# Decoding the weights of an attention kernel with feed-forward to 24 bits: three bitwise steps on VectorE, and the low part by a subtraction on GpSimd

## The chip, the core and the metric

The kernel runs on one core of a Trainium2 chip. The metric is the device time of one launch in microseconds (us), as the median of several runs. A profile of one execution goes with it. TensorE multiplies matrices, VectorE (DVE in the profile), ScalarE (ACT) and GpSimd (POOL) work on vectors, and SyncE (SP) issues the loads and stores. Each engine executes its own instructions in the order in which they stand in its queue, and waits on semaphores for the others.

## What is computed

Linear attention with positive random features for 8 batches, 8 heads, 576 positions and a head dimension of 64, followed by a feed-forward layer on all 4608 tokens of width 512 and inner width 2048. Cut to what matters:

```python
def phi(x):
    proj = np.einsum('bhsd,md->bhsm', x, omega)
    h = proj - np.sum(x * x, axis=-1, keepdims=True) / 2.0
    return np.exp(h - np.max(h, axis=-1, keepdims=True)) / np.sqrt(m)
q_p, k_p = phi(q * scale), phi(k * scale)
kv = np.einsum('bhsm,bhsd->bhmd', k_p, v)
num = np.einsum('bhsm,bhmd->bhsd', q_p, kv)
den = np.einsum('bhsm,bhm->bhs', q_p, k_p.sum(axis=2))[..., None] + 1e-06
x = (num / den).transpose(0, 2, 1, 3).reshape(B * S, H * D)
h = x @ w_in
out = (h - np.tanh(h)) @ w_out
```

The inputs q, k, v and omega are 32-bit floats. The weights `w_in` and `w_out` are 64-bit floats.

## The kernel before

**Tiles.** The inner width of 2048 is cut into 16 chunks of 128 columns, numbered f = 0 to 15. A chunk's weights are 128 partitions by 1024 words of 64 bits: 512 columns of `w_in` and 512 of `w_out`. They come as raw 64-bit words (`raw`, one load of 1 MB each, `fetch`, line 422) and are decoded on the chip, in place, to two 32-bit tiles: a high part `wt[f][:, 0]` and a low part `wt[f][:, 1]`, both in the type fp32r that TensorE multiplies. The products of x and w are made in three passes: xh·wh, xl·wh and xh·wl, where x is split into `xh` and `xl` likewise.

**Order of the work.** 4608 tokens are 18 chunks of 256. At the start the attention of batches 0 and 1 runs: k units (`k_unit`, line 170) make the features of the keys and their sums, q units (`q_unit`, line 319) the features of the queries and a quarter of x each, ending in `x_split` (line 408), which writes a piece of `xh` on ScalarE and of `xl` on VectorE. Eight such pieces (four for each of token chunks 0 and 1) make the x of the first feed-forward pass, which works on both token chunks at once, 512 columns wide. Its step s (`step`, line 545) takes weight chunk s: 12 products into a PSUM tile `h` (line 471), then `g = h - tanh(h)` split into `gh` and `gl` by ScalarE and VectorE (lines 475 to 478), then 12 products into four PSUM tiles (lines 489 to 491). After the 16 steps the remaining token chunks follow, 256 columns wide, with the attention of the later batches in between.

**Decoding.** `decode(f)` (line 427) takes the upper 32 bits of each word (`top`) and 16 middle bits (`mid`). ScalarE writes the absolute value of `top`, seen as a 32-bit float, to a tile `a` (line 438), and 128 times `mid` to a tile `m` (line 440). A clamp (line 442) runs on VectorE for the chunks 0 and 1, on GpSimd for the others. VectorE shifts and masks `a` (line 444), puts in sign and exponent (445), builds the low bits in `m` (448), keeps of `a` the exponent alone (453), and multiplies the two to the low part (454). ScalarE copies `a` to the high part (452). `a` has two buffers, `m` one. The tiles are 128 x 1024.

**What sets the order.** The program is written as one sequence with a count of beats (`t`): a chunk's decode is placed when t reaches 4 + 2.5 f (line 563), and the units by a table. A scheduler of the programming layer (it is on, line 664) then moves instructions of each engine, by its own estimate of when their operands are ready. The loads keep their written order while the first stage runs. The chunks 10 to 15 have their place in memory where the tiles of the first attention stage were, so that their loads follow its end (line 558).

Of the kernel before, what the change touches and what calls it, by code (L numbers as in the profile page):

```python
# [8 lines left out]
F32 = mybir.dt.float32  # L9
F32R = mybir.dt.float32r  # L10
U64 = mybir.dt.uint64
U32 = mybir.dt.uint32
U16 = mybir.dt.uint16
AF = mybir.ActivationFunctionType
ALU = mybir.AluOpType
AX = mybir.AxisListType
# [2 lines left out]
NT, DM, DFF = B * S, H * D, 2048  # L19
P = 128  # L20
# [11 lines left out]
def favor_attention_ffn(ctx: ExitStack, tc: tile.TileContext, qT, kT, va, vt, omT, w, out):  # L32
# [12 lines left out]
    nc = tc.nc  # L45
# [8 lines left out]
    def open_pool(name, side="right"):  # L54
        pools[name] = tc.tile_pool(name=name, bufs=1, side=side, reuse_waits="tile")
        return pools[name].__enter__()
# [37 lines left out]
    dec = open_pool("dec")  # L94
# [318 lines left out]
    wt = {}  # L413

    raws = {}
# [11 lines left out]
    def decode(f):  # L427


        top = raws[f].bitcast(U32)[:, 1::2]  # L430
        topf = raws[f].bitcast(F32)[:, 1::2]
        mid = raws[f].bitcast(U16)[:, 1::4]
        a = dec.tile([P, 2 * DM], U32, tag="a", name=f"a{f}", bufs=2)
        m = dec.tile([P, 2 * DM], U32, tag="m", name=f"m{f}", bufs=1)

        nc.scalar.activation(a.bitcast(F32), topf, AF.Abs)  # L438

        nc.scalar.activation(m, mid, AF.Copy, scale=128.0)  # L440
        engine = nc.vector if f < 2 else nc.gpsimd
        engine.tensor_scalar(a.bitcast(F32), a.bitcast(F32), 2.0**-15, 122879.9921875,  # L442
                             op0=ALU.max, op1=ALU.min)
        nc.vector.tensor_scalar(a, a, 3, 0x3FFFF000, op0=ALU.logical_shift_left, op1=ALU.bitwise_and)
        nc.vector.scalar_tensor_tensor(out=a, in0=top, scalar=0xC0000000, in1=a,
                                       op0=ALU.bitwise_and, op1=ALU.bitwise_or)

        nc.vector.scalar_tensor_tensor(out=m, in0=top, scalar=23, in1=m,
                                       op0=ALU.logical_shift_left, op1=ALU.bitwise_or)

        wt[f] = places[f].tile([P, 2, 2 * DM], F32R, tag=f"w{f}", name=f"w{f}")
        nc.scalar.copy(wt[f][:, 0], a.bitcast(F32))
        nc.vector.tensor_scalar(a, a, 0xFF800000, None, op0=ALU.bitwise_and)
        nc.vector.scalar_tensor_tensor(out=wt[f][:, 1], in0=m, scalar=2.0**-43, in1=a.bitcast(F32),
                                       op0=ALU.mult, op1=ALU.mult)

    xh, xl = [sb.tile([P, 2, NC, TC], F32R, name=f"x{k}") for k in "hl"]
# [95 lines left out]
    while decoded < NF:  # L555
        if t in (2, 4):
            fetch(int(t == 4))
        if not gens and not start and len(places) < NF:
            close_pool("a0")
            weight_places(open_pool("w1", "left"), range(10, NF))  # L560
            for f in range(decoded, decoded + 2):
                fetch(f)
        if decoded in raws and t >= 4 + 2.5 * min(decoded, 16) + 2 * max(0, decoded - 16):
            decode(decoded)
            decoded += 1
            fetch(decoded + 2 - 1)
        if t == 15:
            mode.update(pj=["pj0", "pj1", "po1"], pk=["pk"], pt=["pt", "po0"])
        if done + 2 < decoded and t >= 23 + 1 * done:
            if done == 0:  # L570
                assert xdone[0] == xdone[1] == NC
                out_tiles(0, ("po0", "po1", "pj1", "pt"))
                mode.update(pj=["pj0"], pk=["pk"], pt=["pk"])
            step(done)
            done += 1
        tick(start.pop(t, ()))
        t += 1
# [89 lines left out]
```

## Time and profile before

| | us |
|---|---|
| median of 3 runs | 1066.88 (1065.81 to 1067.43) |
| span of the profiled execution | 1065.4 |
| TensorE products busy in it | 1041.8 (98%) |
| VectorE | 855.5 (80%) |
| ScalarE | 696.4 (65%) |
| GpSimd | 325.9 (31%) |
| weights decoded (first line 438 to last line 454) | 13.0 to 157.7 |

The profiled execution has no other time of its own than its span, from its first instruction to its last; the median of the runs is 1.5 us above it. A row of the profile gives the source line, the engine, the operation, the tile it writes and those it reads, and the shape. In rows with a time in front the first number is the start in us from the start of the span, the second the duration; `[1.06 <-DVE g L476]` says that the engine sat idle for 1.06 us before, until VectorE's `g` of line 476 was done. `min/median/max` are durations in ns. The duration of a VectorE row overlaps the next by about 0.08 us.

### The profile page before, as it was taken

To read this page: it belongs to the slowest core of one execution; us is meant where nothing else is said; L and a number is where in the kernel's file an instruction comes from. 1 tells how busy PE (TensorE), PEld (TensorE's weight loads), DVE (VectorE), ACT (ScalarE), POOL (GpSimd) and SP (SyncE) were. 2 spreads that over 40 slices of the span, in tenths; PEclk is the share of its full clock that TensorE was granted. 3 is DMA by queue.
4 is the path that set the end of the run, shared out by engine and by line. 5 is a ranking of instruction groups with operands and counts; after the bars stand their busy time and mean duration, and the time that the engine had idled before them with its cause. 6 is when DMAs were issued, how large, how long until landed. Compare 5 with 4: busy or idle time off the path is not lost.

```text
span 1065.4 us, 20130 instructions
## 1 busy us (share of the span) xinstructions
PE 1041.8 (98%) x6760; PEld 945.6 (89%) x6760; DVE 855.5 (80%) x2910; ACT 696.4 (65%) x1773; POOL 325.9 (31%) x553
## 2 busy tenths in 40 slices
PE   7988999999999999999999999999999999999998
PEld 7766888999889999999999998999999999999997
DVE  5999995889998886789889878998888887666522
ACT  6997655777677665577777766677767675555422
POOL 4634541344333420133333344333333331000000
PEclk9999999999999999999999999999999999999999
DMA  8750401111111110011111111111101110000000
GB/s 265 237 213 3 187 1 42 53 39 46 31 53 33 54 33 31 11 53 33 53 34 53 34 37 44 33 53 29 47 25 49 33 37 11 30 16 21 1 21 21
DMA packets 35528, 55.90 MB, mean 52 GB/s; under 512 B 12256, under 2 KB 21600, under 8 KB 33376
## 3 DMA queue, kind: packets, MB, share of 16 engines
q1 hardware_dynamic: 35344, 54.57, 16.3%
q8 instruction: 54, 0.88, 0.3%
q14 instruction: 50, 0.41, 0.1%
q10 hardware_dynamic: 80, 0.03, 0.0%
HBM read 45.15 MB, written 9.44 MB: 51 GB/s over the span
## 4 chain that ended last, share of the span: by engine, by line
PE 61%; DVE 2%; ACT 1%; POOL 1%; issue 0%; DVEq 0%; POOLq 0%
PE h L471 26%; PE po L489 8%; PE po L490 8%; PE po L491 8%; PE pj_q L142 2%; PE pk L266 2%; PE pt L366 2%; PE pn L397 1%; PE pn L396 1%; PE pj_kb L142 1%; PE pj_ka L142 1%; PE pk L304 0%; PE pk L302 0%; DVE junk L347 0%; POOL khl L250 0%
## 5 line engine op out<-in xcount | busy, mean ns | idle before, releaser
L471 PE MATMUL h<-xh,w 128*128 128x256 f32 (+1 forms) x2176 | 450.1, 290 | 3.9 <-DVE g L476 2.1
L471 PEld LDWEIGHTS h<-xh,w 128*128 128x128 f32 x2176 | 354.8, 190 | 14.7 <-DVE g L476 3.2
L471 PE MATMUL h<-xl,w 128*128 128x256 f32 (+1 forms) x1088 | 315.8, 290 | 0.0
L489 PE MATMUL po<-w,gh 128*128 128x512 f32 x544 | 213.7, 393 | 0.0
L490 PE MATMUL po<-w,gh 128*128 128x512 f32 x544 | 213.3, 392 | 0.0
L471 PEld LDWEIGHTS h<-xl,w 128*128 128x128 f32 x1088 | 206.9, 190 | 6.0
L491 PE MATMUL po<-w,gl 128*128 128x512 f32 x544 | 209.2, 391 | 0.0
L477 ACT CAST gh<-g 128x512 fp32r<-128x512 f32 x144 | 89.4, 621 | 92.8 <-DVE g L476 91.3
L475 ACT ACTIVATE g<-h 128x512 f32<-128x512 f32 x144 | 85.4, 593 | 95.0 <-PE h L471 82.7
L476 DVE TENSOR_TENSOR g<-h,g 128x512 f32<-128x512 f32 x144 | 98.7, 686 | 57.8 <-ACT g L475 56.6
L478 DVE TENSOR_TENSOR gl<-g,gh 128x512 fp32r<-128x512 f32 x144 | 108.2, 751 | 34.9 <-ACT gh L477 33.1
L491 PEld LDWEIGHTS po<-w,gl 128*128 128x128 f32 x544 | 102.1, 188 | 20.5
L489 PEld LDWEIGHTS po<-w,gh 128*128 128x128 f32 x544 | 102.5, 188 | 16.2
L490 PEld LDWEIGHTS po<-w,gh 128*128 128x128 f32 x544 | 102.5, 188 | 15.3
L347 DVE CUSTOM_DVE_ANT_0 junk<-phi_q,zb 128x128 f32<-128x128 f32 (+1 forms) x320 | 98.5, 309 | 14.4 <-ACT phi_q L150 0.5
L150 ACT ACTIVATE phi_q<-phi_q,nb_q 128x128 f32<-128x128 f32 x240 | 79.6, 392 | 6.8 <-DVE nb_q L146 6.7
L442 POOL TENSOR_SCALAR a<-a 128x1024 f32<-128x1024 f32 x14 | 58.7, 4194 | 54.6 <-ACT a L438 37.2
L250 POOL TENSOR_TENSOR khl<-phi_ka,khl 128x256 fp32r<-128x256 f32 x48 | 37.9, 796 | 121.6 <-DVE khl L249 92.5
L258 POOL CAST vhl<-v 128x128 fp32r<-128x128 f32 (+1 forms) x144 | 45.8, 319 | 91.9 <-PE pk L266 71.5
L390 DVE TENSOR_TENSOR ql<-pt,qh 128x512 fp32r<-128x512 f32 x60 | 41.1, 685 | 32.3 <-ACT qh L389 31.8
L146 DVE CUSTOM_DVE_ANT_0 phi_q<-pj_q,phi_q 128x128 f32<-128x128 f32 x240 | 56.0, 283 | 2.3 <-ACT phi_q L143 2.2
L389 ACT CAST qh<-pt 128x512 fp32r<-128x512 f32 x60 | 34.9, 581 | 32.9 <-PE pt L366 32.6
(152 smaller groups left out, 1938.2 us busy)
## 6 DMA issues: line engine op xcount, KB each, us to landing
raw<-w SPq DMA_DIRECT2D x16, 1024.0 KB, 7.3
kf<-kT SPq DMA_DIRECT2D x32, 288.0 KB, 2.9
qf<-qT SPq DMA_DIRECT2D x72, 128.0 KB, 2.1
out<-o SPq DMA_DIRECT2D x36, 256.0 KB, 2.0
v<-vt SPq DMA_DIRECT2D x24, 288.0 KB, 2.8
v<-va SPq DMA_DIRECT2D x8, 288.0 KB, 5.9
omf<-omT ACTq DMA_DIRECT2D x1, 32.0 KB, 2.2
omf<-omT SPq DMA_DIRECT2D x1, 32.0 KB, 2.4
```

Source lines behind the costliest of these rows:

```text
L146: nc.vector.tensor_tensor_reduce(ph[:, j], pj[:, i, :M], ph[:, j], scale=-SCALE, scalar=3.0e38, op0=ALU.add, op1=ALU.min, accum_out=nb[:, ...
L150: nc.scalar.activation(ph[:, j], ph[:, j], AF.Exp, bias=nb[:, j : j + 1], scale=-1.0)
L347: nc.vector.tensor_tensor_reduce(bank("junk")[r], ph[r, i], kvs[b, c][1][r, h], scale=1.0, scalar=EPS, op0=ALU.mult, op1=ALU.add, accum_ou ...
L442: engine.tensor_scalar(a.bitcast(F32), a.bitcast(F32), 2.0**-15, 122879.9921875, op0=ALU.max, op1=ALU.min)
L471: nc.tensor.matmul(o, w_, x, start=i == 0, stop=i == len(prods) - 1)
L475: nc.scalar.activation(g, p, AF.Tanh)
L476: nc.vector.tensor_sub(g, p, g)
L477: nc.scalar.copy(gh, g)
L478: nc.vector.tensor_sub(gl, g, gh.bitcast(F32))
L489: nc.tensor.matmul(po[t], h, wt[f][:, 0, DM:], start=first, stop=False)
L490: nc.tensor.matmul(po[t], h, wt[f][:, 1, DM:], start=False, stop=False)
L491: nc.tensor.matmul(po[t], l, wt[f][:, 0, DM:], start=False, stop=last)
```

## The change

Only `decode` is changed. The tile `m` and the middle bits go away, and with them ScalarE's second pass (line 440) and VectorE's instructions of the lines 448, 453 and 454. The mask of the shift keeps all bits that the shift leaves. A third bitwise VectorE instruction puts in the three uppermost bits of the lower word (`low`), so that `a` is the weight cut to 24 significant bits. ScalarE's copy rounds it to fp32r as the high part, and the low part is `a` minus that high part: a subtraction on VectorE for the chunks 0 and 1, on GpSimd for the others, 128 x 1024 each. `a` has three buffers instead of two. In the clamp minimum and maximum change places.

```diff
-        mid = raws[f].bitcast(U16)[:, 1::4]
-        a = dec.tile([P, 2 * DM], U32, tag="a", name=f"a{f}", bufs=2)
-        m = dec.tile([P, 2 * DM], U32, tag="m", name=f"m{f}", bufs=1)
-        nc.scalar.activation(a.bitcast(F32), topf, AF.Abs)
-        nc.scalar.activation(m, mid, AF.Copy, scale=128.0)
+        low = raws[f].bitcast(U32)[:, 0::2]
+        a = dec.tile([P, 2 * DM], U32, tag="a", name=f"a{f}", bufs=3)
+        af = a.bitcast(F32)
+        nc.scalar.activation(af, topf, AF.Abs)
         engine = nc.vector if f < 2 else nc.gpsimd
-        engine.tensor_scalar(a.bitcast(F32), a.bitcast(F32), 2.0**-15, 122879.9921875,
-                             op0=ALU.max, op1=ALU.min)
-        nc.vector.tensor_scalar(a, a, 3, 0x3FFFF000, op0=ALU.logical_shift_left, op1=ALU.bitwise_and)
+        engine.tensor_scalar(af, af, 122879.9921875, 2.0**-15, op0=ALU.min, op1=ALU.max)
+        nc.vector.tensor_scalar(a, a, 3, 0x3FFFFFF8, op0=ALU.logical_shift_left, op1=ALU.bitwise_and)
         nc.vector.scalar_tensor_tensor(out=a, in0=top, scalar=0xC0000000, in1=a,
                                        op0=ALU.bitwise_and, op1=ALU.bitwise_or)
-        nc.vector.scalar_tensor_tensor(out=m, in0=top, scalar=23, in1=m,
-                                       op0=ALU.logical_shift_left, op1=ALU.bitwise_or)
+        nc.vector.scalar_tensor_tensor(out=a, in0=low, scalar=29, in1=a,
+                                       op0=ALU.logical_shift_right, op1=ALU.bitwise_or)
         wt[f] = places[f].tile([P, 2, 2 * DM], F32R, tag=f"w{f}", name=f"w{f}")
-        nc.scalar.copy(wt[f][:, 0], a.bitcast(F32))
-        nc.vector.tensor_scalar(a, a, 0xFF800000, None, op0=ALU.bitwise_and)
-        nc.vector.scalar_tensor_tensor(out=wt[f][:, 1], in0=m, scalar=2.0**-43, in1=a.bitcast(F32),
-                                       op0=ALU.mult, op1=ALU.mult)
+        nc.scalar.copy(wt[f][:, 0], af)
+        engine.tensor_sub(wt[f][:, 1], af, wt[f][:, 0].bitcast(F32))
```

The changed kernel's lines up to `decode` have numbers one lower (xl is line 409 instead of 410), those behind it twelve lower. In its `decode` the absolute value is line 434, the clamp 436, the shift 437, the other two bitwise steps 438 and 440, the copy 443 and the subtraction 444.

The scheduler moves the rest. On GpSimd, in the middle of the first attention stage, this stood in a row before (a4 is the `a` tile of chunk 4, and so on; the L442 rows are clamps, `kd` and `vd` small copies of the k units):

```order
L442 TENSOR_SCALAR a4_734<-a4_734 128x1024
L184 COPY kd1_126<-kf_1_3_799 64x64 x2
L185 COPY vd1_127<-v1_125 64x66 x2
L442 TENSOR_SCALAR a5_896<-a5_896 128x1024
L442 TENSOR_SCALAR a6_975<-a6_975 128x1024
L442 TENSOR_SCALAR a7_1072<-a7_1072 128x1024
```

In the changed kernel, from the clamp of chunk 5 to that of chunk 9 (L436 are clamps, L444 subtractions, w3 the weights of chunk 3):

```order
L436 TENSOR_SCALAR a5_881<-a5_881 128x1024
L184 COPY vd0_124<-v0_122 64x66 x2
L444 TENSOR_TENSOR w3_601<-a3_595,w3_601 128x1024
L183 COPY kd1_126<-kf_1_3_784 64x64 x2
L184 COPY vd1_127<-v1_125 64x66 x2
L444 TENSOR_TENSOR w4_728<-a4_722,w4_728 128x1024
L436 TENSOR_SCALAR a6_957<-a6_957 128x1024
L444 TENSOR_TENSOR w5_887<-a5_881,w5_887 128x1024
L436 TENSOR_SCALAR a7_1051<-a7_1051 128x1024
L436 TENSOR_SCALAR a8_1103<-a8_1103 128x1024
L444 TENSOR_TENSOR w6_963<-a6_957,w6_963 128x1024
L436 TENSOR_SCALAR a9_1210<-a9_1210 128x1024
```

The subtractions stand between the clamps, two or three chunks behind them, and the clamp of chunk 5 has come ahead of the copies of the last k unit.

On VectorE, these are the rows from the seventh to the eighth and last `xl` piece of the first two token chunks, before (L454 is the last step of a chunk's decode, here chunk 5; the rest belongs to the attention):

```order
L410 TENSOR_TENSOR xl_101<-pn_0_3_762,xh_100 128x256
L454 SCALAR_TENSOR_TENSOR w5_904<-m5_897,a5_896 128x1024
L350 RECIPROCAL dn_2_1_945<-dn_2_1_945 128x4
L347 ISA junk_65,dn_2_2_1018<-phi_q2_2_1008,zb_1_2_959 128x128
L347 ISA dn_2_2_1018 128x1
L215 TENSOR_TENSOR kvw_1_3_996<-pk_1_3_961,kvw_1_3_996 128x128
L410 TENSOR_TENSOR xl_101<-pn_1_3_872,xh_100 128x256
```

and in the changed kernel (L440 is VectorE's last step of a chunk, here chunk 9):

```order
L409 TENSOR_TENSOR xl_101<-pn_0_3_747,xh_100 128x256
L346 ISA junk1_105,dn_2_2_997<-phi_q2_2_987,zb_0_2_446 64x128
L346 ISA dn_2_2_997 64x1
L214 TENSOR_TENSOR kvw_1_3_975<-pk_1_3_943,kvw_1_3_975 128x128
L349 RECIPROCAL dn_2_1_927<-dn_2_1_927 128x4
L346 ISA junk_65,dn_2_2_997<-phi_q2_2_987,zb_1_2_941 128x128
L346 ISA dn_2_2_997 128x1
L440 SCALAR_TENSOR_TENSOR a9_1210<-raw9_1060,a9_1210 128x1024
L409 TENSOR_TENSOR xl_101<-pn_1_3_857,xh_100 128x256
```

At the same piece of x, VectorE's order had chunk 5 finished and two steps of chunk 6 done before; now it has chunk 9 finished. SyncE's order is unchanged up to the loads of chunk 15.

1 line of the change is left out of this document (removed).

## The prediction

> **What bounds the kernel now.** I read the page's busy times first.
>
> ```profile
> span 1065.4 us, 20130 instructions
> PE 1041.8 (98%) x6760; PEld 945.6 (89%) x6760; DVE 855.5 (80%) x2910; ACT 696.4 (65%) x1773; POOL 325.9 (31%) x553
> ```
>
> TensorE is busy 98% of the span. The work the change takes from VectorE and ScalarE can therefore pay only where TensorE is idle, 1065.4 − 1041.8 = 23.6 us in all. The windows view says where that idle time lies; its columns are the window, its length, and then the busy time and the count of each engine.
>
> ```profile
> 0.00:84.00 84.00, 70.17 (x382) 58.17 (x383) 72.53 (x212) 69.14 (x201) 37.02 (x64) 0.98 0.71 227
> 84.00:100.00 16.00, 13.87 (x75) 11.60 (x74) 15.71 (x42) 12.39 (x24) 8.78 (x2) 1.00 0.01 1
> 100.00:165.00 65.00, 65.00 (x292) 53.61 (x291) 57.66 (x71) 40.88 (x53) 31.23 (x9) 1.00 0.20 80
> 165.00:1066.00 901.00, 892.73 (x6016) 822.23 (x6015) 709.66 (x2588) 573.97 (x1495) 248.83 (x478) 1.00 0.12 35
> ```
>
> TensorE idles 13.8 us before 84 us and 2.1 us up to 100 us; from 100 to 165 us, while the rest of the weights are decoded, it never idles. So a decode that finishes earlier after 100 us is worth nothing, and only the start, where the attention of the first chunks of tokens runs beside the first decodes, is open. Which engine sets the pace there is in the same view of finer windows:
>
> ```profile
> 25.00:50.00 25.00, 23.21 (x132) 19.34 (x132) 25.00 (x68) 24.52 (x74) 16.20 (x15) 1.00 0.82 241
> 50.00:75.00 25.00, 21.07 (x111) 16.59 (x110) 24.95 (x87) 24.58 (x76) 8.20 (x6) 1.00 0.57 195
> 75.00:84.00 9.00, 6.60 (x39) 5.03 (x39) 8.75 (x38) 5.48 (x16) 0.86 (x1) 1.00 0.33 135
> ```
>
> VectorE (third of the busy times) works 58.7 of these 59 us, ScalarE (fourth) nearly as much, GpSimd (fifth) half or less. The feed-forward can start once x is whole, which the `xl` rows of the timeline mark:
>
> ```profile
> 83.04 0.41 DVE L410 TENSOR_TENSOR xl<-pn,xh 128x256 fp32r<-128x256 f32 x1
> ...
> 83.51 0.50 PE L471 MATMUL h<-xh,w 128*128 128x512 f32 x1 [0.23 <-DVE xl L410]
> ...
> 84.98 0.41 DVE L410 TENSOR_TENSOR xl<-pn,xh 128x256 fp32r<-128x256 f32 x1
> ...
> 89.82 0.50 PE L471 MATMUL h<-xh,w 128*128 128x512 f32 x1 [1.06 <-DVE g L476]
> ...
> 97.93 0.50 PE L471 MATMUL h<-xh,w 128*128 128x512 f32 x1 [1.07 <-DVE g L476]
> ```
>
> At 83 to 85 us VectorE writes the last two of the eight `xl` pieces, TensorE takes them up at once, and then waits only twice more, both times for VectorE. VectorE is an in-order engine that is full, so the sum of what stands ahead of the eighth `xl` in its order sets when TensorE becomes full. That is the number I forecast.
>
> **VectorE's own decode work ahead of that point.** The decode rows of VectorE up to 84 us, grouped (count, busy us, mean ns):
>
> ```profile
> L445 DVE SCALAR_TENSOR_TENSOR a<-raw,a 128x1024 uint32<-128x1024 uint32 x7 | 8.5, 1215 | 0.0
> L448 DVE SCALAR_TENSOR_TENSOR m<-raw,m 128x1024 uint32<-128x1024 uint32 x6 | 8.2, 1360 | 0.0
> L454 DVE SCALAR_TENSOR_TENSOR w<-m,a 128x1024 fp32r<-128x1024 uint32 x6 | 7.3, 1215 | 0.0
> L444 DVE TENSOR_SCALAR a<-a 128x1024 uint32<-128x1024 uint32 x7 | 4.8, 686 | 0.1
> L453 DVE TENSOR_SCALAR a<-a 128x1024 uint32<-128x1024 uint32 x6 | 4.2, 692 | 0.0
> L442 DVE TENSOR_SCALAR a<-a 128x1024 f32<-128x1024 f32 x2 | 1.4, 694 | 0.8 <-ACT a L438 0.8
> ```
>
> These are 34.4 us for six whole chunks and the start of a seventh, the same 34 instructions that the order has ahead of the eighth `xl`. The removed instructions (L453, L454) and the new third one (a SCALAR_TENSOR_TENSOR like L445) make a chunk 2 × 1.215 + 0.686 = 3.1 us where it was 3 × 1.215 + 0.686 + 0.692 = 5.0. But the order of the changed kernel has ten whole chunks ahead of the same `xl`. That is 10 × 3.1 = 31.2, plus the two clamps, 1.4, plus the two subtractions of chunks 0 and 1, which stay on VectorE. The nearest row for one of them is L454, also 1024 elements to fp32r: 2 × 1.215 = 2.4. Sum 35.0 us, and from the 34.4 I take 0.9 first, by which the six L448 exceed 1215 ns (that is waiting, treated below): **+1.5 us**. So the saving on VectorE is spent on decoding four chunks earlier than TensorE needs them. ScalarE, by the same count, has 10 absolute values and 9 copies there, where it had 7 absolute values, 6 middle words and 6 copies: 19 and 19, no gain.
>
> **What GpSimd's subtractions cost VectorE.** No row of before has GpSimd subtract 1024 columns. The nearest rows, durations as min/median/max in ns:
>
> ```profile
> L250 POOL TENSOR_TENSOR khl<-phi_ka,khl x48: 727/742/1311, 179.7 to 872.3; 128x256 fp32r<-128x256 f32 x48
> L272 POOL TENSOR_TENSOR zs<-zt x48: 452/508/950, 186.9 to 886.6; 128x128 f32<-128x128 f32 x48
> L249 DVE CAST khl<-phi_ka x48: 263/287/844, 179.2 to 871.4; 128x256 fp32r<-128x256 f32 x48
> L442 POOL TENSOR_SCALAR a<-a x14: 3622/4180/4645, 26.4 to 146.4; 128x1024 f32<-128x1024 f32 x14
> L448 DVE SCALAR_TENSOR_TENSOR m<-raw,m x16: 1204/1217/2057, 15.5 to 153.0; 128x1024 uint32<-128x1024 uint32 x16
> L162 DVE TENSOR_REDUCE nb_k<-pj_k x16: 673/679/692, 6.7 to 64.8; 128x4 f32<-128x512 f32 x16
> ```
>
> By the minima, 128 more columns of a GpSimd tensor-tensor take 727 − 452 = 275 ns, so 1024 columns take 0.73 + 6 × 0.275 = 2.38 us (estimate from L250 and L272; between 2.4 and the 4.2 of the clamp). VectorE is held meanwhile. The timeline has one L448 that starts 0.41 us after a clamp does:
>
> ```profile
> 34.53 3.98 POOL L442 TENSOR_SCALAR a<-a 128x1024 f32<-128x1024 f32 x1 [1.53 <-issue]
> ...
> 34.94 2.06 DVE L448 SCALAR_TENSOR_TENSOR m<-raw,m 128x1024 uint32<-128x1024 uint32 x1
> ```
>
> The L448 takes 2.06 us instead of 1.22: 0.84 us held by a GpSimd read of 1 × 1024 columns. The cast L249 that runs beside the subtraction L250 reaches 0.84 instead of 0.29: 0.56 us held by a read of 2 × 256. L162, which reads PSUM, never varies, so an instruction between may hide part. Scaled by columns like its length, the hold of a subtraction of 2 × 1024 is up to 0.56 + 6 × 0.275 = 2.2 us; twice the clamp's would be 1.7; with PSUM readers in front it can be 0. I take 1.3, three quarters of the 1.7. GpSimd's order has the subtractions of chunks 2 to 8 ahead of the point, seven: **+9.1 us** (0 to 15.4). The order also has the clamps of chunks 2 to 9 there, eight, where before has five:
>
> ```profile
> 0.00:85.00 85.00, 1.39 (x2) 19.85 (x5) 0.98 0.70 224
> ```
>
> (the window of L442 alone; POOL is the last pair.) Three more at up to 0.84: **+1.5** (0 to 2.5).
>
> The Trainium skill, page "SBUF — State Buffer", section "Who interferes with whom", says more: GpSimd shares a port pair with VectorE, and a VectorE instruction with two SBUF inputs, or in a two-port mode, is fully blocked until a GpSimd instruction that reads SBUF and started first is finished. The clamp rows disagree as to the whole length (4.18 us long, 0.84 held); the L250 rows come closer (0.56 of 0.74). By that rule each subtraction would hold VectorE 2.38 us, seven 16.7 us, and the sum below would be 17.6 instead of 10.0.
>
> **What is won.** After the point, before still decodes on VectorE between the `g` rows, and TensorE loses the 2.1 us of the 84:100 window. In the changed order no decode stands there until chunk 10, whose words cannot be loaded before the attention's tiles are free: **−1.5** (0 to −2.1). In the first 25 us VectorE has gaps that an earlier chunk can fill: **−0.6** (0 to −1).
>
> **Edits that I cost at nothing.** All that leaves ScalarE and VectorE after 100 us: TensorE is full there. The third `a` buffer lifts the wait of ScalarE's absolute value, which nothing waits for there either. The six subtractions of chunks 10 to 15 hold VectorE too, but TensorE then has a product of another step to do, and if that cover is gone each costs at most 2.2 us. GpSimd's small copies `kd` and `vd` queue behind more, at the worst a clamp and a subtraction, 6.6 us; what waits for them is a projection whose result VectorE, full as it is, takes up late anyway. Without that cover this goes to the high end. SP issues the same loads in the same order up to chunk 15. Swapping min and max in the clamp: the same row. TensorE's order differs in places up to the 2,059th of its 6,760 products and is then the same; up to there I take ±1 us.
>
> **Sum:** 1.5 + 9.1 + 1.5 − 1.5 − 0.6 = +10.0 us on the profiled execution, 1065.4 to 1075.4 us. The runs' median, 1066.88, lies 1.5 us above that span, so I forecast 1066.9 + 10 = **1076.9 us**. A measurement of this kernel tells about 0.2%, 2.1 us, from no change.
>
> **Rivals.**
> - *A, the forecast:* the subtractions hold VectorE in its full stage. Between 1071 and 1085 us. Chance 0.64.
> - *B, the holds fall on instructions that wait anyway or read PSUM:* then 1.5 − 2.1 − 1 = −1.6 to about +2, 1065 to 1069 us. For it: L162 is untouched by GpSimd and makes up 19 of the 84 us. Against: the L448 and L249 maxima. Chance 0.15: 0.06 faster, 0.06 the same, 0.03 slower.
> - *C, faster:* the attention stage is set by VectorE's work per chunk and not by where the scheduler put the chunks: six chunks × 1.9 us saved, less 2.4 for two subtractions, is 9.1 us of the 13.8 that TensorE idles, 1058 us. It decides if VectorE's decode instructions let attention pass, that is, if fewer than about eight chunks are really decoded before the eighth `xl`. Against it: VectorE executes in the order shown. Chance 0.13.
> - *D, much slower:* GpSimd becomes the bound of the decode, and TensorE waits for weights after 100 us. A chunk costs GpSimd 4.2 + 2.4 = 6.6 us. The rows
>
> ```profile
> 109.83 4.30 POOL L442 TENSOR_SCALAR a<-a 128x1024 f32<-128x1024 f32 x1 [2.65 <-ACT a L438]
> ```
> ```profile
> L454 DVE SCALAR_TENSOR_TENSOR w<-m,a x16: 1204/1217/1253, 22.8 to 156.5; 128x1024 fp32r<-128x1024 uint32 x16
> ```
>
> say that before clamps chunk 10 at 109.8 and finishes chunk 15 at 157.7 with TensorE full, so six chunks may take 47.9 us, 8.0 each, before anyone waits. At 8.6 each (a subtraction as slow as the clamp) that costs 4 us more, with the holds near their upper end 1085 to 1092 us. Chance 0.08.
>
> **How the numbers follow.** Faster: C and part of B, 0.19. The same: part of B and A's low edge, 0.09. Slower: A, D and the rest, 0.72. The range runs from 1064, B's low end, to 1085, A's high end; C and D's upper half, about 0.17, stay outside.
>
> **What would show it.** Right: in the changed profile the eighth `xl` at about 95 us; TensorE idle before it about 24 instead of 14 us, and full after; a GpSimd subtraction row (its line 444) of about 2.4 to 3 us; VectorE's bitwise rows of two tensors (its lines 438 and 440) with maxima of 3 us and more. Wrong: `xl` at 85 us or earlier (B, C), or TensorE waiting for `w` from GpSimd after 100 us (D).

## The result and the profile after

The changed kernel takes 1091.03 us (median of 4 runs, 1089.32 to 1091.52) against 1067.16 us for the kernel before on the same chip: 1.0221 times, 95% interval 1.0207 to 1.0236. That is 23.9 us more, where 10.0 were forecast, and above the forecast's range. Slower was right; the size was not. In the profiled execution the span grew from 1065.4 to 1089.4 us:

```profile
span 1089.4 us, 20108 instructions
...
PE 1054.3 (97%) x6760; PEld 956.0 (88%) x6760; DVE 859.0 (79%) x2880; ACT 681.4 (63%) x1757; POOL 323.5 (30%) x567
```

The work went down as announced, on ScalarE by 15.0 us and on GpSimd by 2.4, but VectorE, which lost 30 instructions, is busy 3.5 us longer, and TensorE's idle time is 35.1 us instead of 23.6. The windows say where (window, length, busy time and count of PE, PEld, DVE, ACT, POOL, then the granted clock):

```profile
25.00:50.00 25.00, 19.62 (x97) 16.85 (x97) 24.39 (x54) 20.36 (x58) 12.87 (x20) 0.86 0.73 212
50.00:75.00 25.00, 20.78 (x98) 16.91 (x98) 25.00 (x67) 19.44 (x61) 9.76 (x9) 0.80 0.37 130
75.00:84.00 9.00, 4.31 (x18) 3.10 (x16) 9.00 (x23) 6.93 (x21) 3.87 (x2) 0.86 0.68 249
84.00:100.00 16.00, 10.92 (x45) 9.09 (x44) 14.96 (x43) 8.16 (x19) 6.43 (x3) 0.76 0.19 67
100.00:125.00 25.00, 21.71 (x112) 18.19 (x113) 12.62 (x41) 9.91 (x23) 2.38 (x1) 1.00 0.00 1
125.00:165.00 40.00, 38.61 (x171) 30.83 (x170) 30.37 (x28) 19.45 (x26) 18.60 (x10) 1.00 0.32 127
```

Read the third busy column against its count. From 50 to 84 us VectorE works all 34 us, as before, but gets 90 instructions done where it did 125. The TensorE column falls with it, and from 100 to 165 us, where TensorE was always busy before, it now idles 4.7 us. The rows of the decode, by tile (count, then min/median/max in ns, first and last start in us):

```profile
L437 DVE TENSOR_SCALAR a<-a x16: 675/681/1525, 15.7 to 168.1; 128x1024 uint32<-128x1024 uint32 x16
L438 DVE SCALAR_TENSOR_TENSOR a<-raw,a x16: 1205/1226/3409, 17.1 to 168.8; 128x1024 uint32<-128x1024 uint32 x16
L440 DVE SCALAR_TENSOR_TENSOR a<-raw,a x16: 1208/1213/3306, 19.1 to 170.6; 128x1024 uint32<-128x1024 uint32 x16
...
L436 POOL TENSOR_SCALAR a<-a x14: 1029/1090/2021, 24.0 to 159.0; 128x1024 f32<-128x1024 f32 x14
L444 POOL TENSOR_TENSOR w<-a,w x14: 2348/2401/2966, 38.3 to 174.6; 128x1024 fp32r<-128x1024 f32 x14
```

The subtraction's own length, 2.40 us, is the 2.38 of the prediction. What to look at is the maximum of VectorE's rows: 3.4 us for an instruction whose median is 1.2. The timeline has one:

```profile
58.15 2.37 POOL L444 TENSOR_TENSOR w<-a,w 128x1024 fp32r<-128x1024 f32 x1 [3.99 <-ACT w L443]
...
58.21 3.39 DVE L438 SCALAR_TENSOR_TENSOR a<-raw,a 128x1024 uint32<-128x1024 uint32 x1
```

L438 started 0.06 us behind the subtraction and took 3.39 us instead of 1.21: it was held 2.18 us, nearly the subtraction's whole length. The Trainium skill, page "SBUF — State Buffer", section "Who interferes with whom", says that a VectorE instruction with two SBUF inputs is blocked until a GpSimd instruction that reads SBUF and started first is finished; this row agrees (2.18 of the 2.31 us that the subtraction had left).

The row of the `xl` pieces gives the starts of the first and of the eighth (51.6 and 103.2). The eighth is the point that the prediction named as the one that decides:

```profile
L409 DVE TENSOR_TENSOR xl<-pn,xh x8: 406/410/425, 51.6 to 103.2; 128x256 fp32r<-128x256 f32 x8
```

103.2 us instead of 85.0, so 18.2 of the 24.0 us stand there; the forecast for this point was +11.5. For each VectorE instruction ahead of it I take its duration less the usual one of its form (the first quartile). These excesses sum to 4.0 us in before and to 17.7 us now. Of the latter, 12.8 us lie beside the seven subtractions (1.25, 1.87, 2.18, 2.11, 2.09, 2.15 and 1.18) and 4.8 in seven rows beside clamps (before: 4.0, also in seven rows). All these rows lie beside GpSimd instructions. A wait of VectorE for TensorE would show as idle time instead, and ahead of the point VectorE idles 12.9 us where it idled 11.5.

Behind the point 5.8 us more are lost, where the forecast had a gain of 1.5. The first wait of TensorE there, in the timeline of all engines:

```profile
104.39 2.38 POOL L444 TENSOR_TENSOR w<-a,w 128x1024 fp32r<-128x1024 f32 x1 [6.10 <-ACT w L443]
...
104.53 2.38 DVE L346 CUSTOM_DVE_ANT_0 junk<-phi_q,zb 64x128 f32<-64x128 f32 x1
...
107.26 0.69 ACT L354 ACTIVATE phi_q<-phi_q,dn 128x128 f32<-128x128 f32 x2 [2.37 <-DVE dn L349]
...
108.11 0.60 ACT L463 ACTIVATE g<-h 128x512 f32<-128x512 f32 x1
...
109.46 0.68 DVE L464 TENSOR_TENSOR g<-h,g 128x512 f32<-128x512 f32 x1
...
110.20 0.50 PE L459 MATMUL h<-xh,w 128*128 128x512 f32 x1 [3.27 <-DVE g L464]
```

A subtraction holds an attention row of VectorE (2.38 us instead of 0.29); ScalarE's next attention step waits 2.37 us for what follows it; the tanh of the feed-forward stands behind that step on ScalarE, `g` behind the tanh, and TensorE waits 3.27 us. Most of this comes back: TensorE's lag (defined below) goes from 18.2 to 20.4 us at this wait and is 18.8 us by the 520th product, because before waited for `g` here twice, 1.06 and 1.07 us. The rest of the 5.8 us is lost later, and e6, e9 and e10 bear on it. GpSimd itself is idle most of the time: it holds up three engines with 2.4 us of work.

### The profile page after: what moved, and what is told of

It reads as the page before. It is cut to its first block, busy times and chain, and to the rows that moved or that the text cites. A ratio compares the mean times of both kernels' runs of the same rounds, so it can differ in the third digit from the quotient of the medians.

```text
span 1089.4 us, 20108 instructions
## 1 busy us (share of the span) xinstructions
PE 1054.3 (97%) x6760; PEld 956.0 (88%) x6760; DVE 859.0 (79%) x2880; ACT 681.4 (63%) x1757; POOL 323.5 (30%) x567
## 4 chain that ended last, share of the span: by engine, by line
PE 60%; DVE 3%; issue 1%; POOL 0%; ACT 0%; DVEq 0%
PE h L459 25%; PE po L477 8%; PE po L478 8%; PE po L479 8%; PE pj_q L141 2%; PE pk L265 2%; PE pt L365 2%; PE pn L396 1%; PE pn L395 1%; PE pj_kb L141 1%; PE pj_ka L141 1%; DVE junk L346 0%; PE pk L303 0%; PE pk L301 0%; DVE phi_q L145 0%
## 5 line engine op out<-in xcount | busy, mean ns | idle before, releaser
L464 DVE TENSOR_TENSOR g<-h,g 128x512 f32<-128x512 f32 x144 | 98.9, 687 | 62.4 <-ACT g L463 61.1
L346 DVE CUSTOM_DVE_ANT_0 junk<-phi_q,zb 128x128 f32<-128x128 f32 (+1 forms) x320 | 106.0, 334 | 14.8 <-ACT phi_q L149 0.5
L257 POOL CAST vhl<-v 128x128 fp32r<-128x128 f32 (+1 forms) x144 | 48.3, 337 | 84.9 <-PE pk L265 71.2
L249 POOL TENSOR_TENSOR khl<-phi_ka,khl 128x256 fp32r<-128x256 f32 x48 | 38.1, 800 | 115.2 <-DVE khl L248 107.3
L365 PE MATMUL pt<-ident,phi_q 128*128 128x128 f32 x288 | 45.7, 280 | 10.5 <-DVE xl L409 6.8
```

The source lines that it names most:

```text
L346: nc.vector.tensor_tensor_reduce(bank("junk")[r], ph[r, i], kvs[b, c][1][r, h], scale=1.0, scalar=EPS, op0=ALU.mult, op1=ALU.add, accum_ou ...
L365: nc.tensor.transpose(pt[:, i * P : (i + 1) * P], ph[:, ix(i // 2, i % 2)], ident)
L464: nc.vector.tensor_sub(g, p, g)
```

## The experiments

Three measures are used. The **point** is the start of the eighth `xl` piece, from its row (85.0 us in before); the expectations call it the eighth difference. The **lag** is the start of the k-th of TensorE's 6,760 products less that of the k-th in before; at the 520th product, 114 us in before, it tells what the point has cost, and at the last ones what the kernel has cost. The times are medians, their ratio is to the kernel before on the same chip. The granted clock and the early order differ a little from kernel to kernel, and single runs of one kernel lie up to 6 us apart, so differences under some 4 us between two of these kernels are not read unless their intervals tell them apart.

| kernel | point, us | lag at 114 us | lag at the end | time, us | ratio (95%) |
|---|---|---|---|---|---|
| changed kernel | 103.2 | +18.8 | +24.5 | 1091.0 | 1.0221 (1.0207–1.0236) |
| e1 memset in place of the subtraction | 87.4 | −0.9 | −0.8 | 1067.9 | 1.0010 (0.9999–1.0021) |
| e2 one operand read | 91.9 | +6.6 | +6.7 | 1072.6 | 1.0050 (1.0034–1.0066) |
| e3 old clamp in the changed kernel | 101.7 | +18.9 | +24.8 | 1092.2 | 1.0238 (1.0222–1.0253) |
| e4 new clamp in the kernel before | 85.4 | +0.4 | +0.2 | 1066.8 | 0.9996 (0.9986–1.0005) |
| e5 one operand read, behind the copy | 92.9 | +4.2 | +4.5 | 1071.3 | 1.0035 (1.0022–1.0048) |
| e6 two buffers | 93.8 | +7.7 | +7.4 | 1074.3 | 1.0063 (1.0048–1.0078) |
| e7 subtraction on VectorE | 96.8 | +9.4 | +9.5 | 1077.4 | 1.0091 (1.0074–1.0108) |
| e8 the same, two buffers | 82.4 | +0.6 | +0.6 | 1067.6 | 1.0002 (0.9992–1.0011) |
| e9 late memset | 101.6 | +18.9 | +18.9 | 1087.1 | 1.0190 (1.0162–1.0218) |
| e10 early memset | 91.3 | +3.3 | +7.6 | 1074.2 | 1.0062 (1.0044–1.0081) |
| e11 one buffer | 80.4 | −7.0 | +54.6 | 1122.2 | 1.0518 (1.0502–1.0535) |
| e12 one buffer, VectorE | 72.6 | −14.1 | +34.7 | 1102.4 | 1.0334 (1.0317–1.0350) |
| e13 later decode | 93.6 | +5.3 | +21.6 | 1087.7 | 1.0188 (1.0165–1.0211) |
| e14 latest decode | 83.2 | −3.2 | +20.3 | 1087.7 | 1.0196 (1.0181–1.0211) |
| e15 later decode, VectorE | 82.8 | −1.4 | +2.3 | 1071.2 | 1.0044 (1.0027–1.0061) |
| e16 latest decode, VectorE | 79.2 | −9.3 | +2.8 | 1070.8 | 1.0044 (1.0029–1.0059) |
| e17 one buffer, then two | 78.0 | −2.2 | −2.3 | 1064.3 | 0.9979 (0.9971–0.9988) |
| e18 the same, later | 80.0 | −7.9 | −2.3 | 1064.7 | 0.9974 (0.9966–0.9983) |

The theory on trial (T1, holds): GpSimd's reads hold VectorE ahead of the point. Rivals: the early decode of four more chunks by itself, and GpSimd's own length or its place in the chain.

### Is it the reads?

**e1**, the subtraction of chunks 2 to 15 replaced:

```diff
-        engine.tensor_sub(wt[f][:, 1], af, wt[f][:, 0].bitcast(F32))
+        if f < 2:
+            engine.tensor_sub(wt[f][:, 1], af, wt[f][:, 0].bitcast(F32))
+        else:
+            nc.gpsimd.memset(wt[f][:, 1].bitcast(F32), 0.0)
```

> GpSimd's subtraction of chunks 2 to 15 is replaced by a GpSimd memset of the low part (it only writes; the low parts of these chunks are left out of the computation). VectorE's order keeps ten chunks ahead of the eighth xl piece. Theory 1 (VectorE is held while GpSimd reads its two operands): the seven holds of 1.83 us go, so the eighth xl comes 12.8 us earlier, near 90 us, and the time falls from 1091 to about 1076 us, the smaller waits behind 150 us included. Rival 2 (the early decode of four more chunks alone, whatever GpSimd does): nothing moves, 1089 to 1092 us. Rival 3 (GpSimd's queue makes others late): a memset of unknown length, so between the two, with waits for POOL in the rows of ScalarE or TensorE.

Measured: 1067.9 us, the kernel before's time, and the point at 87.4 us with the same ten chunks ahead of it. The early decode by itself costs nothing that can be told, and the whole 24 us go with the subtraction; T1's own number, about 1076 us, was too timid. More than the reads goes with it: the memset is shorter (1.09 us in the mean) and does not wait for ScalarE's copy. e2 and e5 leave one read and differ in that wait; e3 and e4 change GpSimd's length alone.

**e2**, as e1, with the last line reading the decoded word only:

```diff
+            nc.gpsimd.tensor_scalar(wt[f][:, 1], af, 0.0, 1.0, op0=ALU.mult, op1=ALU.mult)
```

> GpSimd's subtraction of chunks 2 to 15 is replaced by a GpSimd tensor_scalar that reads the one tile a (the low parts of these chunks are zero, left out of the computation). Theory 1: a hold is set by the columns read, 1024 instead of 2048, so at most 0.84 instead of 2.2 us and about 0.7 in the mean; seven times 1.1 us less is 8 us, the eighth xl near 95 us, the time 1081 to 1084 us, between the memset and the subtraction. Rival 2: 1089 to 1092 us.

Measured: 1072.6 us, below the range that T1 gave. The instruction is 1.1 us long (its group's mean) and its holds over the whole run sum to 5.7 us, against 23.2 us for the fourteen subtractions:

```profile
L447 POOL TENSOR_SCALAR w<-a 128x1024 fp32r<-128x1024 f32 x14 | 15.6, 1114 | 39.8 <-DVE a L440 27.6 <-issue 9.7 <-DVE dn L349 1.2
```

With a quarter of the holds about a quarter of the loss is left. It does not go in strict proportion: the memsets of e1 hold VectorE for 4.8 us too, and cost nothing that can be told. And of the 4.5 us between the points of e1 and e2, 2.0 are idle time of VectorE (10.0 us in e1, 12.0 in e2), not holds.

**e5** reads ScalarE's copy instead, and so waits for it as the subtraction does:

```diff
+            nc.gpsimd.tensor_scalar(wt[f][:, 1], wt[f][:, 0].bitcast(F32), 0.0, 1.0, op0=ALU.mult, op1=ALU.mult)
```

> For chunks 2 to 15 GpSimd writes the low part as zero times the high part: one operand read instead of two, but the operand is ScalarE's copy, so GpSimd still waits for that copy as the subtraction does (the low part is left out of the product). Holds: as in the kernel that read only the decoded word, about 0.6 us for each of the seven instead of 1.83, so 1070 to 1075 us. Rival, the wait: if the later place in GpSimd's queue (behind ScalarE's copy), and not the reads, delays the next chunk and VectorE behind it, the time stays at 1085 to 1092 us.

Measured: 1071.3 us. The wait for ScalarE's copy, which e1 and e2 had taken away as well, costs nothing that these two tell apart. The rival "place in the chain" falls.

**e3** and **e4**, the clamp's two orders exchanged between the kernels:

```diff
-        engine.tensor_scalar(af, af, 122879.9921875, 2.0**-15, op0=ALU.min, op1=ALU.max)
+        engine.tensor_scalar(af, af, 2.0**-15, 122879.9921875, op0=ALU.max, op1=ALU.min)
```

> The changed kernel with the clamp's two operations in the old order (maximum first); every engine's order of instructions is the same. Theory 1: GpSimd's clamp takes 4.2 instead of 1.1 us again, but holds VectorE no longer than the 0.84 us of its reads, so the eighth xl stays at 103 us within 1 us and the time within 2 us of 1091. Rival 3 (what counts is how long GpSimd is busy): 8 clamps of 3.1 us more ahead of the point make it 5 to 25 us slower, 1096 to 1115 us.

> The kernel before with only the clamp's two operations exchanged (minimum first); every engine's order is the same. Theory 1: the clamp falls from 4.2 to about 1.1 us, its hold of VectorE stays, the time stays within 2 us of 1067. Rival 3: GpSimd's small copies and the decode come earlier, 1 to 6 us faster, 1061 to 1066 us.

Measured: 1092.2 and 1066.8 us, no change either way, though the instruction's length changes by more than 2 us. The first row is of e3, whose clamp has maximum first, the second of e4, whose clamp has minimum first:

```profile
L436 POOL TENSOR_SCALAR a<-a x14: 3622/3699/4594, 23.1 to 160.6; 128x1024 f32<-128x1024 f32 x14
```
```profile
L442 POOL TENSOR_SCALAR a<-a x14: 1040/1636/2507, 27.5 to 146.7; 128x1024 f32<-128x1024 f32 x14
```

GpSimd's length as such is no cause: in e3 it is busy 363.0 us instead of 323.5, with nothing to show for it.

### Where on VectorE's road?

**e6**, two buffers for `a` instead of three (the changed kernel's subtraction):

```diff
-        a = dec.tile([P, 2 * DM], U32, tag="a", name=f"a{f}", bufs=3)
+        a = dec.tile([P, 2 * DM], U32, tag="a", name=f"a{f}", bufs=2)
```

> The changed kernel with two buffers for the decoded words instead of three: eight chunks instead of ten are decoded ahead of the eighth difference of the product, by the order. Holds: five subtractions instead of seven and two chunks of VectorE's work less ahead of it, 2 x (1.83 + 2.9) = 9.5 us earlier there, 3 to 5 of them given back behind it, so 1080 to 1087 us. Rival, early decode alone: two of the four extra chunks gone, half of the 24 us, 1077 to 1081 us. Were three buffers needed to cover a chain of waits between the engines, it would be slower than 1091.

Measured: 1074.3 us. The point came 9.4 us earlier, as worked out (9.5):

```profile
L409 DVE TENSOR_TENSOR xl<-pn,xh x8: 386/412/417, 43.5 to 93.8; 128x256 fp32r<-128x256 f32 x8
```

But nothing was given back behind it; the changed kernel's loss of 5.7 us there went as well. So the time was missed by 6 us, in the part behind the point. Nine of e6's fourteen GpSimd subtractions start behind the point, and TensorE's lag does not grow there (7.7, then 7.4).

**e7**, the subtraction on VectorE for all chunks:

```diff
-        engine.tensor_sub(wt[f][:, 1], af, wt[f][:, 0].bitcast(F32))
+        nc.vector.tensor_sub(wt[f][:, 1], af, wt[f][:, 0].bitcast(F32))
```

> The changed kernel with the subtraction on VectorE for all chunks: GpSimd's reads of two operands are gone, VectorE does ten subtractions of 1.22 us (measured on chunks 0 and 1) ahead of the eighth difference instead of two. Holds: there VectorE pays 8 x 1.22 = 9.8 us in place of 12.8 us of holds, so the eighth difference starts 1 to 5 us earlier than at 103.2 us and the time is 1080 to 1090 us. Rival, GpSimd's queue (its length or its waits set the pace, not VectorE): GpSimd is relieved of 2.4 us per chunk, 1067 to 1075 us.

Measured: 1077.4 us, 2.6 us under the expected range, the point at 96.8. VectorE does the subtraction itself in 1.2 us and is better off than when GpSimd does it for it in 2.4 us. **e8** has both edits of e6 and e7:

> As the kernel with the subtraction on VectorE, with two buffers for the decoded words: by the order 8 shifts, 8 sign merges, 7 low-bit merges and 7 subtractions stand ahead of the eighth difference, 8 x 0.60 + 8 x 1.13 + 7 x 1.13 + 7 x 1.13 = 29.7 us of VectorE's time, against about 34 us in the kernel before, and no reads of GpSimd there but the clamps'. Holds: the eighth difference at 82 to 87 us and the time 1063 to 1070 us. Early decode alone: two of four extra chunks remain, about 1078 us.

Measured: 1067.6 us, the point at 82.4: as T1 has it, level with the kernel before.

**e9** and **e10** split e1: memset for the chunks 10 to 15 alone (condition `f < 10` for the subtraction), and for 2 to 9 alone (`f < 2 or f >= 10`).

> GpSimd subtracts for chunks 2 to 9, and for chunks 10 to 15 a memset stands in the subtraction's place (their low part is left out). Holds: the eighth difference stays at 101 to 104 us and TensorE's lag there at about 19 us; the waits of the feed-forward products for g and its low part between 150 and 161 us (2.4 us) go with the late reads, so 1086 to 1089 us; the 3 us more between 318 and 385 us, where nothing is decoded, go or stay with the order. Rival: the late subtractions are what costs (on GpSimd they pass on to later weights), and without them the time falls under 1080 us.

> The other half: memset for chunks 2 to 9 (low part left out), GpSimd subtracts for chunks 10 to 15 only. Holds ahead of the point: the eighth difference at 86 to 89 us as in the kernel with memsets throughout, and the time 1066 to 1070 us, the up to 2.4 us of waits between 150 and 161 us included. Rival (late subtractions): over 1075 us.

Measured: 1087.1 and 1074.2 us. With memsets for the six late chunks nothing more is lost behind the point (lag 18.9 and 18.9); with subtractions for these alone 4.3 us are (3.3, then 7.6). I had priced the late subtractions at nothing; here 4 to 6 us go with them. By their times alone e9 and the changed kernel are not told apart (the intervals overlap), e10 and e1 are. It is no fixed price of a subtraction: e6 has nine behind the point and loses nothing there. In the changed kernel's lag 2.4 us of the late loss come up at 151 to 161 us, among held decode rows, and 3 us only between 318 and 385 us, where nothing is decoded. The latter too are absent in e9, but there the subtractions are not all that differs. The scheduler gave e9 another order: 1057 of TensorE's products between the 616th and the 2,235th (415 us in the changed kernel) are not the ones that stand at the same place in the changed kernel, while e10 has the changed kernel's order from the 471st on. Whether these 3 us come from the reads or from the order, no run tells.

e10's time missed its range, half by this and half by a point at 91.3 us where 86 to 89 were expected. Up to 120 us e10 and e1 have the same instructions in the same order on TensorE, VectorE, ScalarE and GpSimd, so the edit does not explain the 3.9 us between their points. 3.6 of them are idle time of VectorE (13.7 us ahead of the point against 10.0), and TensorE's granted clock differs. Two windows of e1, then the same of e10 (the clock is the third number from the right):

```profile
25.00:50.00 25.00, 21.88 (x121) 18.25 (x122) 25.00 (x71) 23.65 (x70) 13.09 (x21) 1.00 0.85 248
75.00:84.00 9.00, 7.55 (x44) 6.07 (x45) 8.85 (x32) 5.31 (x16) 0.95 (x1) 1.00 0.10 44
```
```profile
25.00:50.00 25.00, 20.41 (x105) 17.91 (x104) 24.36 (x65) 21.77 (x64) 10.98 (x20) 0.86 0.73 220
75.00:84.00 9.00, 6.97 (x29) 5.26 (x28) 8.89 (x30) 7.12 (x19) 2.98 (x3) 0.70 0.43 154
```

In the first 25 us it is the other way round (0.93 in e1, 1.00 in e10). That the clock makes the difference was not tried alone; a difference of this size between the points of two kernels need not come from their edits.

### Is it the place or the work?

**e11** (one buffer, GpSimd's subtraction) and **e12** (one buffer, VectorE's) leave five chunks ahead of the point; the edits are those of e6 and e7 with `bufs=1`.

> The changed kernel, the subtraction on GpSimd as it is, with one buffer for the decoded words instead of three: five chunks ahead of the eighth difference by the order instead of ten, three GpSimd subtractions at most. Holds: two chunks less brought the point from 103.2 to 93.8 us, three more less bring it to 80 to 85 us, and what is early there is no gain under some 88 us, so the point alone gives 1064 to 1068 us; but with one buffer a chunk's chain (absolute value, clamp, three steps on VectorE, copy, subtraction: 1.1 + 1.1 + 3.0 + 1.1 + 2.4 us and the hand-overs, about 10 us) is longer than TensorE's step per chunk of 5.4 us, and eleven chunks are left: up to 11 x 4.6 us would be missing less the lead of the decode; so 1066 to 1100 us. If the time is near the kernel before, the lead covers it.

> One buffer and the subtraction on VectorE: five chunks and four subtractions ahead of the eighth difference, about 19 us of VectorE's time there against 34 in the kernel before. Holds: the point at 72 to 80 us, no gain from it below some 88 us as the kernel with two buffers and VectorE's subtraction showed (82.4 us, same time as before), so 1064 to 1068 us if the chain of one buffer (about 9 us a chunk) is covered, later if TensorE comes to wait for weights. Rival, that the point still sets the time below 85 us: 1055 to 1060 us.

Measured: 1122.2 and 1102.4 us, both above what was expected. At 114 us both were ahead of the kernel before, by 7.0 and 14.1 us; so, against what I had read from e8, a point earlier than 85 us does set TensorE free earlier. Then the decode starved it. The waits of TensorE in e11 from 100 to 200 us (what waited, for what, us in total, times, longest):

```profile
PE po L477 <- ACT gh L465: 14.4, 7, 2.1
PE h L459 <- POOL w L444: 7.4, 6, 1.7
```

Neither separates the place of the subtraction from the supply of weights.

**e13** and **e14** keep all instructions and the three buffers of the changed kernel and place the decode later in the program, every 4.0 and every 5.0 beats:

```diff
-        if decoded in raws and t >= 4 + 2.5 * min(decoded, 16) + 2 * max(0, decoded - 16):
+        if decoded in raws and t >= 4 + 4.0 * min(decoded, 16) + 2 * max(0, decoded - 16):
```

> All instructions and the three buffers of the changed kernel, the decode of a chunk every 4 beats of the program instead of every 2.5: by the order seven chunks ahead of the eighth difference instead of ten, and chunk 7 comes after the sixth feed-forward step's difference g. Holds and place: three chunks and three subtractions less, 3 x (2.9 + 1.83) = 14 us earlier, the point near 89 us and the time 1066 to 1073 us. Rival, the work itself (wherever the sixteen subtractions stand they hold VectorE, and TensorE pays later): 1080 to 1091 us.

> The same with a chunk every 5 beats: six chunks ahead of the eighth difference, the point at 83 to 87 us. Chunks 6 to 8 then follow the sixth step's g, with about one step of lead against a chain of some 10 us per chunk, so TensorE may wait up to 10 us for weights near 115 to 125 us: 1064 to 1076 us. Rival, the work itself: over 1080 us.

Measured: 1087.7 us both, by T1's numbers a miss. At 114 us e14 is 3.2 us ahead, with the point at 83.2 us, but by the end it is 20.3 behind. The timeline between, where the decode now stands beside the feed-forward:

```profile
119.73 2.90 POOL L444 TENSOR_TENSOR w<-a,w 128x1024 fp32r<-128x1024 f32 x1 [2.24 <-ACT w L443]
...
120.46 3.25 DVE L440 SCALAR_TENSOR_TENSOR a<-raw,a 128x1024 uint32<-128x1024 uint32 x1
...
123.80 1.05 ACT L443 CAST w<-a 128x1024 fp32r<-128x1024 f32 x1 [4.15 <-DVE a L440]
...
124.89 0.59 PE L459 MATMUL h<-xh,w 128*128 128x512 f32 x1 [4.37 <-ACT w L443]
```

The subtraction of one chunk holds VectorE's last step of the next (3.25 us instead of 1.21), ScalarE's copy waits for it, and TensorE, with no chunk in hand, waits 4.37 us. The hold makes up 2.0 of these; the rest I put down to the late place itself. e16 below has this place without these holds and loses 12.1 us behind 114 us, where e14 loses 23.5. T1's clause "ahead of the point" falls: the holds are paid where the decode has no lead, on either side of it.

**e15** (every 3.5 beats) and **e16** (every 5.0), with the subtraction on VectorE as in e7:

> Subtraction on VectorE, three buffers, a chunk every 3.5 beats: eight shifts, seven of each merge and six subtractions ahead of the point, 27.4 us of VectorE's work there against about 34 in the kernel before: the point near 80 to 84 us. Two buffers with 29.7 us gave 82.4 us and no gain. Place: 1063 to 1069 us; a gain over the kernel before only if the point still sets the time below 85 us (then 1061 to 1064).

> Subtraction on VectorE, three buffers, a chunk every 5 beats: six chunks with six subtractions ahead, the point at 74 to 80 us, and unlike the kernel with one buffer three buffers to supply the rest (4 us of VectorE per chunk against 5.4 of TensorE). TensorE led by 14 us at 120 us in the one-buffer kernel; up to 8 us of this may be lost at chunk 6, which comes after the sixth g. Place: 1055 to 1064 us, faster than both. Rival: waits for weights eat the lead, 1066 to 1080 us.

Measured: 1071.2 and 1070.8 us, both above what the place was expected to give. e16 against e14 is the plainest pair: the same place in the program, the subtraction on the one engine or the other, 1070.8 against 1087.7 us. Of their difference 6.1 us stand at 114 us. e16 was 9.3 us ahead at 114 us, but chunk 6 came too late behind the sixth step and the lead went, as the rival had it. The waits of TensorE from 60 to 400 us, two of the rows:

```profile
PE h L459 <- DVE g L464: 3.0, 3, 1.3
PE h L459 <- DVE w L444: 2.9, 2, 1.8
```

**e17** gives the first six chunks one buffer and the others two of their own, so that little stands ahead of the point and the rest has its lead; subtraction on VectorE as in e7. **e18** is the same at 3.5 beats.

```diff
-        a = dec.tile([P, 2 * DM], U32, tag="a", name=f"a{f}", bufs=3)
+        a = dec.tile([P, 2 * DM], U32, tag="a" if f < 6 else "b", name=f"a{f}", bufs=1 if f < 6 else 2)
```

> One buffer for the words of chunks 0 to 5, two others for chunks 6 to 15, subtraction on VectorE, a chunk every 2.5 beats: by the order seven shifts, six of each merge and five subtractions ahead of the eighth difference (23.2 us of VectorE's work, against about 34 in the kernel before), and chunks 7, 8 and 9 behind the first, second and third feed-forward step instead of the sixth. Point and supply: the point at 76 to 80 us, TensorE ahead of the kernel before by 5 to 10 us at 110 us and no wait for weights behind it: 1057 to 1063 us, faster than both. Rival: the decode of nine chunks behind the point delays g on VectorE and eats the lead, 1065 to 1071 us.

> The same with a chunk every 3.5 beats: six shifts, six and five merges and five subtractions ahead, chunks 6 and 7 behind steps 1 and 3. Point and supply: 1 to 3 us earlier at the point, the lead of chunks 8 and later a step shorter: 1056 to 1064 us. Rival: as there, 1065 to 1073 us.

Measured: 1064.3 and 1064.7 us, faster than the kernel before by 0.21% and 0.26% (intervals 0.9971 to 0.9988 and 0.9966 to 0.9983), and by some 26 us faster than the changed kernel; the gain expected was larger (at least 4 and 3 us), and both lie just above their ranges. The windows of e17:

```profile
0.00:84.00 84.00, 72.19 (x402) 59.97 (x402) 72.17 (x213) 66.74 (x201) 22.88 (x66) 1.00 0.71 227
84.00:100.00 16.00, 15.27 (x68) 11.79 (x68) 15.47 (x38) 9.68 (x19) 2.87 (x2) 0.89 0.00 1
100.00:165.00 65.00, 63.77 (x286) 52.72 (x287) 47.74 (x59) 31.02 (x45) 9.55 (x8) 1.00 0.22 85
```

TensorE does 402 products by 84 us where it did 382, and idles 2.0 us from there to 165 us (2.1 in before). Its lead, 4.9 us at the product that starts at 84 us in before, is 2.2 us at the 520th; the clock of the second window is 0.89, and whether that takes the rest was not tried. e18 was 7.9 us ahead at 114 us and lost 5.5 of it between 236 and 370 us, when all weights were decoded; what takes it there was not tried.

## Why the prediction was right in kind and wrong in size

**Right.** The point that decides, the ten chunks ahead of it, the length of the subtraction (2.38 forecast, 2.40 median) and the holding of VectorE as the main cause: e1 takes away the subtraction and with it the whole loss, e2 and e5 one of its two reads and with it most of the loss.

**The sum, term by term**, on the span:

| term | forecast | measured |
|---|---|---|
| VectorE's own work ahead of the point | +1.5 | +1.6, and 1.5 more that I cannot assign to rows |
| holds by seven subtractions | +9.1 | +12.8 |
| more clamps | +1.5 | +0.8 |
| idle time of VectorE ahead of the point | −0.6 | +1.4, none of it in the first 25 us |
| behind the point | −1.5 | +5.8 |
| sum | +10.0 | +24.0 |

**The step that failed first** is the choice of 1.3 us per subtraction, "three quarters of the 1.7", out of 0 to 2.2. The measured mean is 1.83, and four of seven were over 2.0. I had let PSUM readers such as L162 stand in front; but that row was 19 of the 84 us and most others could be held. The row nearest in kind was L249 beside L250, another two-operand GpSimd instruction, which gave the 2.2; I weighed the clamp's row as much, which reads one operand. The Trainium skill's rule of "SBUF — State Buffer" (the whole instruction blocked) had given a sum of 17.6 us, 7.6 nearer to the result; its seven times 2.38 are more than the 12.8 measured, so part of its closeness came from the other terms.

**The step that failed most** is the part behind the point: 7.3 of the 14.0 us missed. It held a gain of 1.5 us, and it put the six late subtractions at nothing because "TensorE then has a product of another step to do". The gain came, but behind a larger loss: the lag rises by 2.2 us at the wait of 3.27 us shown above and falls by 1.6 up to the 520th product. The cover was read from before, where TensorE never idled from 100 to 165 us; but there no GpSimd instruction held VectorE for over 0.86 us, and the cover of one step was just enough. In the changed kernel it failed for 2.4 us at 151 to 161 us, and in e10 likewise; in e6 it held. The other 3 us, at 318 to 385 us, stay open, as said at e9: the late subtractions, or the order of TensorE's products. The prediction took that order to be the same as before from the 2,059th product on; in the traces it differs up to the 2,235th (390 us in before).

**The idle time of VectorE** grew, and TensorE's granted clock fell with TensorE's idling: 0.80 from 50 to 75 us and 0.76 from 84 to 100 us in the changed kernel, 1.00 in these windows of before. TensorE's products take 12.5 us longer in all. Ahead of the point this is a small part of the loss, since VectorE's idle time grew by only 1.4 of the 18.2 us there; behind it, from 100 to 165 us, the clock is 1.00. The clock was not tried alone; e14 lost 20.3 us with a mean clock of 0.996.

**The rivals.** B (holds hidden) and C (work per chunk) fall with the point at 103 us; C's mechanism is alive where fewer chunks stand ahead, in e17. D (GpSimd as the bound) has the right time, 1085 to 1092 us, for the wrong reason: e3 makes GpSimd 39.5 us busier at no cost. Two slips in the working change nothing: C's saving adds up to 9.0 us, not 9.1, and the range begins 1 us under B's low end.

**The clamp**, "the same row", is no such thing: 4.18 us became 1.09. It mattered to nothing, as e4 shows.

## What to carry to other kernels

Price work that is handed to GpSimd by what it holds on VectorE, not by its own length: a two-operand instruction of 2.4 us on an engine idle 70% of the time cost more than the 1.2 us for which VectorE does it itself. And when instructions become cheaper, ask how many more of them a scheduler with one more buffer will put ahead of what the slowest engine waits for. Cover that was read from a profile holds for waits of the size that this profile has.

## What the runs showed of the hardware

**The order of a clamp's two operations.** On GpSimd, 128x1024 floats, maximum then minimum takes 3.6 to 4.6 us, minimum then maximum 1.03 to 2.51 us; e3 differs from the changed kernel, and e4 from the kernel before, in nothing else. Why, no run tells. Both hold VectorE for at most 0.86 us, so the long form holds it for a fifth of its length only.

**A write holds some instructions too.** In e1 the memset reads nothing. Its timeline:

```profile
42.51 0.95 POOL L447 MEMSET w<- 128x1024 f32 x1
...
42.52 0.28 DVE L346 CUSTOM_DVE_ANT_0 junk<-phi_q,zb 128x128 f32<-128x128 f32 x1
...
50.13 0.95 POOL L447 MEMSET w<- 128x1024 f32 x1
...
50.15 1.48 DVE L437 TENSOR_SCALAR a<-a 128x1024 uint32<-128x1024 uint32 x1
```

The two-operand L346 beside the first keeps its 0.28 us; the one-operand L437 beside the second takes 1.48 us instead of 0.68. Of the seven L346 rows of e1 that start during a memset six take 0.28 us or less; the seventh (34.09 us, 0.85 us) stands right behind a `tensor_scalar` that was held itself. By the section of the Trainium skill's page "SBUF — State Buffer" named above, a GpSimd instruction that only writes leaves two-input instructions alone, while a `tensor_scalar` in a two-port mode contends with any; the two rows agree, if L437 runs in such a mode, for which its 0.68 us against the 1.21 of the two-operand rows of its size speaks.

**Instructions that PSUM feeds were not held.** In e3 three of the eight L409 rows (`xl<-pn,xh`, one operand from PSUM) lie beside subtractions, and the longest of the eight takes 0.43 us; three `g` rows (L464, one operand from PSUM) start during a subtraction there and keep their 0.69 us. L346, L438 and L440 were held there by up to 2.2 us.
